# Token mix in 24 steps of all 512 channels, with products of 512 and 256 columns, in one fixed order that begins inside the attention's last units

## The chip, the core and the metric

The kernel runs on one core of one Trainium2 chip. The metric is the device time in microseconds (us) of one execution. The core's engines are TensorE (PE in the profile, its weight loads PEld), VectorE (DVE), ScalarE (ACT), GpSimd (POOL) and SyncE (SP, here only an issuer of DMAs). Each engine works through its own list of instructions in order and waits on semaphores for the others.

## The reference, cut to what matters

```python
scores = where(mask, q @ k.T / sqrt(64), -1e9)        # [4, 8, 768, 768], blocks of 32
x      = softmax(scores) @ v                          # attention, then [4, 768, 512]
theta  = x @ w_theta                                  # [4, 768, 512]
y      = w_tok_r @ (x * cos(theta)) + w_tok_i @ (x * sin(theta))   # mixes the 768 tokens
u      = x + y
out    = u + maximum(u @ w_ch, 0)
```

The mask keeps a window of three blocks, the first and the last block, and three sampled blocks for each block of queries. All inputs are float32.

## The kernel before, in words

**Attention.** The function `attention` runs over 56 units (two pairs of batches, each 6 units for the two edge blocks and 22 for the inner blocks), in an order that is written out by hand under a manual schedule. One unit has scores on PE (L315), row maxima on DVE (L323), exponentials on ACT (L341), transposes on PE (L351), their copies out of PSUM on ACT (L357), and products with the values on PE (L373, tile `X`); units overlap by a software pipeline, so that step n does the scores of unit n+1 and the values of unit n-1. The results go to a DRAM tile `xs` (L400). Weights arrive as 64-bit words; a `Decoder` turns them into a high and a low float32r part in "pieces": one activation and one cast on ACT (L63, L81) and seven DVE instructions (L68, L69, L70, L76, L78, L85, L86). A number of shares of pieces is due in each step of the attention; `theta`, all of `tok_r` and two thirds of `tok_i` are decoded there.

**Mix.** The function `token_mix` is a generator. It yields to the attention at its first loads, and then, in the attention's last step, at its first products. Everything after that is written in program order and put into its order on each engine by a scheduler of the framework that has a timeline of its own. There are 48 steps k: four batches b, two halves h of the 512 channels, six blocks j of 128 tokens. Each step loads `xa` (the block, turned) by four DMAs (L526); every other step loads `xr` (L537), turns it on DVE (`turn`, L553) and splits it into `xT` high and low (L554, L555). `theta(k)` makes 12 products of 256 columns (L563 to L565) into a PSUM tile `h`, and from it an angle between -pi and pi (ACT L567, L568; DVE L570 to L572) and its cosine and sine (ACT L574 to L576). `turned(k)` multiplies by `xa` (DVE L585) and splits both results into `zh` and `zl` (ACT L588, DVE L589). `mix(k)` makes 24 products of 384 columns (L601 to L603) into four PSUM tiles `y`, each of which collects all six blocks of its half. After j = 5, `add_x` adds x and splits the sum into `uh`, `ul` (DVE L614, L615, L617, ACT L616). `out` makes 12 products of 384 columns (L624 to L626), two DVE instructions (L629, L630) and a store; there are 32 of them, eight after each batch, those of the last batch at the very end. The 14 last pieces (six of 256 columns of `tok_i`, eight of `ch`) are decoded in the first steps of the mix. High and low parts mean three products for each full one: high by high, high by low, low by high.

**What is waited for around the change.** The pools of the mix (`zp`, `tp1`, `wk`, `up`, `ps_y`) lie where the attention's pools were, so their first use waits until those are released; `xp`, `tz` and `tp0` lie on the right side, in the place of the attention's early pools.

## Time and profile before

| | |
|---|---|
| median of 3 runs | 649.26 us (642.14 to 651.48) |
| the profiled execution | 649.64 us, of which 647.6 us are the span of its records |
| last value product of the attention starts | 286.50 us after the span's start |
| first product of `mix` | 306.97 us |
| last product of `out` starts | 643.49 us |

Busy time counts from the first to the last instruction of the span. Matmuls are pipelined, so the distance between the starts of two neighbours says more of PE's pace than the duration of one. The granted clock (PEclk) tells how much of full speed PE was given.

### The profile page before, as it was taken

Reading aid. Unit: us, or ns where it says so; the run is one execution under the profiler, and the core shown is the slowest. Engines: PE = TensorE matmul, PEld = TensorE weight load, DVE = VectorE, ACT = ScalarE, POOL = GpSimd, SP = SyncE. Lnnn points to the kernel's source line nnn. Section 1 sums busy time; section 2 is a strip of 40 time slices with the busy share of each in tenths; the row PEclk is TensorE's granted clock in tenths of the full one; section 3 lists DMA queues with packets and bytes.
Section 4 is the critical chain, followed back from the end, with each engine's and each line's share of the span. In section 5 each row is a group of like instructions: output and inputs, shape, how many; then the busy total and the mean of one; then the engine's idle time right before and its main releaser. Section 6 shows DMA issues by size and latency. Waiting matters only on the chain.

```text
span 647.6 us, 19671 instructions
## 1 busy us (share of the span) xinstructions
PE 560.7 (87%) x7936; PEld 489.0 (76%) x7936; DVE 460.6 (71%) x1207; ACT 356.8 (55%) x844; POOL 131.4 (20%) x230
## 2 busy tenths in 40 slices
PE   2788687698877787865999999999999999999997
PEld 1455465465555555654898989999999999999997
DVE  4677746568898677776889899674784857746554
ACT  1866666567866576754556655355552456424520
POOL 1248534352196454500000000000000000000000
PEclk9988988899988898987999999999999999999999
DMA  8937989968799788864442233311142211221002
GB/s 315 312 94 222 271 249 250 264 172 255 243 244 241 207 246 230 245 168 137 132 131 85 80 86 120 116 65 46 54 139 78 68 49 35 74 68 61 28 2 97
DMA packets 71098, 96.82 MB, mean 150 GB/s; under 512 B 5600, under 2 KB 52832, under 8 KB 70624
## 3 DMA queue, kind: packets, MB, share of 16 engines
q1 hardware_dynamic: 63488, 68.04, 35.6%
q0 software_dynamic: 4928, 17.57, 10.4%
q10 hardware_dynamic: 2592, 9.96, 5.1%
q8 instruction: 62, 1.02, 0.7%
q14 instruction: 28, 0.23, 0.1%
HBM read 82.97 MB, written 12.58 MB: 148 GB/s over the span
## 4 chain that ended last, share of the span: by engine, by line
PE 68%; DMA 13%; DVE 8%; issue 7%; ACT 3%; SPq 1%; DVEq 0%; ACTq 0%
PE X L373 8%; PE y L601 8%; PE y L603 8%; PE y L602 8%; PE S L315 7%; PE T L351 6%; PE o L624 3%; PE o L626 3%; PE o L625 3%; DMA raw_ch<-in_w_ch_dram 3%; PE h L565 2%; PE h L564 2%; PE h L563 2%; DMA xs<-xo 2%; PE X_w L373 2%
## 5 line engine op out<-in xcount | busy, mean ns | idle before, releaser
L601 PE MATMUL y<-w_second,zh 128*128 128x384 f32 x288 | 96.5, 335 | 1.2 <-ACT zh L588 1.2
L602 PE MATMUL y<-w_second,zh 128*128 128x384 f32 x288 | 96.3, 334 | 0.0
L603 PE MATMUL y<-w_second,zl 128*128 128x384 f32 x288 | 91.9, 334 | 0.0
L357 ACT COPY pT<-T 128x512 f32<-128x512 f32 x88 | 48.1, 590 | 60.6 <-PE T L351 59.3
L341 ACT ACTIVATE P<-S,nm 128x256 f32<-128x256 f32 x176 | 69.0, 476 | 11.0 <-DVE nm L325 10.0
L323 DVE TENSOR_REDUCE m<-S 128x2 f32<-128x512 f32 x88 | 56.6, 685 | 19.7 <-PE S L315 16.5
L373 PE MATMUL X<-vb,pT 128*32 128x65 f32 (+1 forms) x1408 | 58.5, 234 | 12.9 <-issue 11.9
L315 PE MATMUL S<-kg,q 64*32 64x256 f32 x1408 | 59.2, 405 | 10.5 <-issue 9.2
L373 PE MATMUL X<-va,pT 128*32 128x65 f32 (+1 forms) x1408 | 52.6, 237 | 14.4 <-DMA va<-in_vr_dram 5.1
L563 PE MATMUL h<-w_theta_hi,xTh 128*128 128x256 f32 x192 | 55.5, 289 | 10.5 <-ACT xTh L554 10.5
L351 PEld LDWEIGHTS T<-ident,P 128*128 128x128 f32 x352 | 42.0, 151 | 28.0 <-issue 14.1
L351 PE MATMUL T<-ident,P 128*128 128x128 f32 x352 | 56.7, 301 | 7.2 <-issue 5.7
L373 PEld LDWEIGHTS X<-va,pT 128*32 128x32 f32 (+1 forms) x1408 | 37.0, 117 | 26.2 <-issue 12.0
L565 PE MATMUL h<-w_theta_hi,xTl 128*128 128x256 f32 x192 | 55.7, 290 | 1.0 <-DVE xTl L555 1.0
L294 POOL DMA_INDIRECT vb<-in_vr_dram,rows x44 | 49.3, 1120 | 33.6 <-PE X_w L373 25.6
L601 PEld LDWEIGHTS y<-w_second,zh 128*128 128x128 f32 x288 | 54.1, 188 | 1.6 <-ACT zh L588 1.6
L373 PEld LDWEIGHTS X<-vb,pT 128*32 128x32 f32 (+1 forms) x1408 | 41.6, 119 | 17.9 <-issue 17.4
L564 PE MATMUL h<-w_theta_lo,xTh 128*128 128x256 f32 x192 | 55.1, 287 | 0.0
L602 PEld LDWEIGHTS y<-w_second,zh 128*128 128x128 f32 x288 | 54.1, 188 | 0.0
L603 PEld LDWEIGHTS y<-w_second,zl 128*128 128x128 f32 x288 | 53.7, 188 | 0.0
L567 ACT ACTIVATE t<-h,up_int 128x256 f32<-128x256 f32 x48 | 22.5, 472 | 48.1 <-PE h L565 40.9
L563 PEld LDWEIGHTS h<-w_theta_hi,xTh 128*128 128x128 f32 x192 | 37.5, 195 | 11.3 <-ACT xTh L554 11.3
(145 smaller groups left out, 1317.0 us busy)
## 6 DMA issues: line engine op xcount, KB each, us to landing
xa<-xs SPq DMA_DIRECT2D x192, 64.0 KB
va<-in_vr_dram SPq DMA_DIRECT2D x30, 260.0 KB
xr<-xs SPq DMA_DIRECT2D x24, 256.0 KB
out_dram<-of SPq DMA_DIRECT2D x32, 192.0 KB
q<-in_qT_dram SPq DMA_DIRECT2D x22, 256.0 KB
xs<-xo SPq DMA_DIRECT2D x44, 128.0 KB
raw_tok_r<-in_w_tok_r_dram ACTq DMA_DIRECT2D x8, 576.0 KB
va<-in_vr_dram SPq DMA_DIRECT2D x30, 130.0 KB
```

What stands on the lines that cost most here:

```text
L294: nc.gpsimd.indirect_dma_start(out=vb[0:96], out_offset=None, in_=vr, in_offset=bass.IndirectOffsetOnAxis(ap=tab.rows[:, bp, i : i + 1], a ...
L315: nc.tensor.matmul(sc[32 * p : 32 * p + 32, e, b, :], q[rows, b, p, :], keys[rows, :, 4 * b + p, :], start=True, stop=True)
L323: nc.vector.tensor_reduce(m[:, 2 * e : 2 * e + 2], sc[:, e], axis=AX.X, op=ALU.max)
L341: nc.scalar.activation(pt[:, e, b], sc[:, e, b], AF.Exp, bias=nm[:, 2 * e + b : 2 * e + b + 1], scale=0.125)
L351: nc.tensor.transpose(banks[k // 4][:, k % 4], pt[:, (k // 2) % 2, k % 2, 128 * (k // 4) : 128 * (k // 4) + 128], ident)
L373: nc.tensor.matmul(s["X"][32 * p : 32 * p + 32, b, e, :], s["T"][0:rows, 4 * c + 2 * e + b, 32 * p : 32 * p + 32], v[0:rows, v0 : v0 + 65] ...
L563: nc.tensor.matmul(ps, hi[:, c, :], wh[:, c, :], start=c == 0, stop=False)
L564: nc.tensor.matmul(ps, hi[:, c, :], wl[:, c, :], start=False, stop=False)
L565: nc.tensor.matmul(ps, lo[:, c, :], wh[:, c, :], start=False, stop=c == 3)
L601: nc.tensor.matmul(acc, zh[:, dd], wh[:, tt], start=j == 0 and m == 0, stop=False)
L602: nc.tensor.matmul(acc, zh[:, dd], wl[:, tt], start=False, stop=False)
L603: nc.tensor.matmul(acc, zl[:, dd], wh[:, tt], start=False, stop=j == 5 and m == 1)
```

## The change

In words:

- The mix has 24 steps (four batches, six blocks), each of all 512 channels. `theta(k)` is 12 products of 512 columns: first the eight with the high part of x, then the four with the low part. `mix(k)` is, for each of four blocks c of 128 channels, six pairs of products: 512 columns into a PSUM tile `ya` of its own, and 256 columns into a half of a PSUM tile `yb`, which the blocks 0 and 1, and the blocks 2 and 3, share. `out` is 12 pairs likewise, and for the last batch the eight outs stand side by side, with c as the outer loop.
- `xT` stays float32, and the high and low part of a block live in two short tiles. `add_x` adds in place (two DVE instructions of 512 and 256 columns), then one cast of 768 columns on ACT and one subtraction of 768 on DVE. `finish` is one DVE instruction instead of two.
- The whole mix is under a manual schedule: on each engine the instructions stand as the code has them. In step k stand `theta(k+2)`, the sines of k+1, `turn(k+3)`, the multiplications and splits of k+1, the integer and reduction of k+2, then 2, 2, 1, 1, 2, 1, 4, 1 pieces in the steps 0 to 7, then `mix(k)`, with four outs of the batch before between its second and third block of channels in the steps j = 1 and j = 2.
- The attention's early pools are released four units before its end, and the generator is called seven times from there to the last unit: raw loads, turns and splits of blocks 0 to 2, `theta(0)`, `theta(1)` and the reduction of block 0 stand inside the last units. The pieces of the attention are due four units before its end instead of one.
- The first two `xa` loads and the raw loads of all 14 last pieces are issued by GpSimd; before, SP issued them. The last outs are stored from SP (512 columns) and ACT (256).
- `xp`, `tz` and the raw tiles of the last pieces lie in the attention's main pools now.

The diff, cut to its core:

```diff
-                    due = 3 * len(early_pieces) + 3 * len(late_pieces) * (n - half) // (steps - 2 - half)
+                    due = 3 * len(early_pieces) + 3 * len(late_pieces) * (n - half) // (len(units) - 4 - half)
...
                 do(n - 1, values)
+                if len(units) - 2 <= n < len(units):
+                    next(follow)
                 do(n, evict)
...
+                if n == len(units) - 4:
+                    early.close()
+                if len(units) - 4 <= n < len(units):
+                    next(follow)
...
-        steps = 12 * nb
+        steps = 6 * nb
+        halves = ((0, 512), (512, 256))
...
-        def mix(k):
-            b, h, j = at(k)
+        def mix(k, between):
+            b, j = at(k)
             if j == 0:
-                ys[b, h] = [ps_y.tile([P, 384], F32, tag="y", name=f"y{k}_{a}") for a in range(4)]
-            for a in range(4):
+                two = [ps_y.tile([P, 2, 256], F32, tag=f"yb{x}", name=f"yb{b}_{x}") for x in range(2)]
+                ys[b] = [(ps_y.tile([P, 512], F32, tag=f"ya{c}", name=f"ya{b}_{c}"), two[c // 2][:, c % 2, :]) for c in range(4)]
+            for c in range(4):
...
+                if j == 5:
+                    add_x(b, c)
+                if c == 1:
+                    between()
...
+        def add_x(b, c):
...
+            u = xT[b][:, c, :]
+            for (t0, n), acc in zip(halves, ys[b][c]):
+                nc.vector.tensor_tensor(u[:, t0 : t0 + n], acc, u[:, t0 : t0 + n], op=ALU.add)
+            uh, ul = [t[:, c, :] for t in us[b]]
+            nc.scalar.copy(uh, u)
+            nc.vector.tensor_tensor(ul, u, uh.bitcast(F32), op=ALU.subtract)
...
+        def finish(b, e, t0, n, ps, queue):
+            o = wk.tile([P, 512], F32, tag="o", name=f"of{b}_{e}_{t0}")[:, :n]
+            nc.vector.scalar_tensor_tensor(o, ps, 0.0, xT[b][:, e, t0 : t0 + n], op0=ALU.max, op1=ALU.add)
+            queue.dma_start(outT[b, 128 * e : 128 * e + 128, t0 : t0 + n], o)
...
+        with tc.manual_schedule():
+            load(0, nc.gpsimd)
+            for piece in rest[:2]:
+                piece.load(stage, nc.gpsimd)
+            load(1, nc.gpsimd)
+            load_raw(4)
+            theta(2)
+            sines(0)
+            times(0)
+            split(0)
+            integer(1)
+            reduce(1)
+            load(2)
+
+            shares = [2, 2, 1, 1, 2, 1, 4, 1]
...
```

**PE at the attention's end** (tile names: `T` transposes, `X` value products, `h` the theta products, `xh` and `xl` the parts of x; the number behind `X_` is the block). Before, the last two units follow each other:

```order
L373 MATMUL X_20_5417<-vb_115,pT_20_5364 32x65 x4
L351 MATMUL T_22_0_5503<-ident,P_22_5453 128x128 x4
L351 MATMUL T_22_1_5504<-ident,P_22_5453 128x128 x4
L373 MATMUL X_21_5513<-va_113,pT_21_5450 32x65 x4
L373 MATMUL X_21_5513<-vb_116,pT_21_5450 32x65 x4
```

Now `theta(0)` stands between them, and `theta(1)` likewise ahead of `X_22`:

```order
L568 MATMUL h_5512<-w_theta_hi,xh_5482 128x512
L569 MATMUL h_5512<-w_theta_lo,xh_5482 128x512
L571 MATMUL h_5512<-w_theta_hi,xl_5483 128x512 x4
L351 MATMUL T_22_0_5532<-ident,P_22_5489 128x128 x4
L351 MATMUL T_22_1_5533<-ident,P_22_5489 128x128 x4
L373 MATMUL X_21_5542<-va_116,pT_21_5486 32x65 x4
```

What moved: 12 products of 512 columns ahead of the last transposes, and 12 more ahead of the last value products.

**GpSimd behind the attention's last gather** (`vb` are gathered values, `xa` the mix's blocks, `raw` the undecoded weights; what an instruction waits for is in brackets, DMAHW and DMASW being DMAs of the hardware and the software queues). Before, nothing follows:

```order
L259 COPY kg_110<-k_182 128x256 [waits Pool_49]
L294 DMA vb_116<-in_vr_dram,rows 96x1040 [waits DMASW6_49]
L294 DMA vb_117<-in_vr_dram,rows 96x1040 [waits DMASW7_49,PE_49]
L797 UNCONDITIONAL_BRANCH
L797 ISA [waits barrier_Pool_Activation_PE_DVE_SP_gather]
```

Now:

```order
L294 DMA vb_120<-in_vr_dram,rows 96x1040 [waits DMASW7_49,PE_49]
L535 DMA xa_5690<-xs 128x1x128 [waits DMAHW1_49,DMAHW0_49,DMAHW2_49,DMASW3_49,DMAHW3_49,DMASW2_49,DMAHW4_49,DMASW1_49,DMAHW5_49,DMASW0_49,DMAHW6_49,PE_49,DMAHW7_49,Activation_49,Pool_49]
L535 DMA xa_5690<-xs 128x1x128 x3
L58 DMA raw_tok_i_5695<-in_w_tok_i_dram 128x512
L58 DMA raw_tok_i_5697<-in_w_tok_i_dram 128x512
L535 DMA xa_5699<-xs 128x1x128 x2
```

What moved: eight `xa` loads and the raw loads came from SP's list to the end of GpSimd's. The first of them waits for PE's last value product `X_22`, since its tile lies in a pool that the attention releases as a whole.

**PE at the end of a batch, step 5, j = 5** (`y`, `ya`, `yb` are the sums in PSUM). Before, the four sums take turns and none waits for DVE's add:

```order
L601 MATMUL y_3_5816<-w_second,zh_5_6063 128x384
L602 MATMUL y_3_5816<-w_second,zh_5_6063 128x384
L603 MATMUL y_0_5813<-w_second,zl_5_6064 128x384 [waits DVE_49]
L603 MATMUL y_1_5814<-w_second,zl_5_6064 128x384
L603 MATMUL y_2_5815<-w_second,zl_5_6064 128x384
L603 MATMUL y_3_5816<-w_second,zl_5_6064 128x384
```

Now a block of channels is finished before the next begins:

```order
L627 MATMUL ya_0_5809<-w_second,zl_5_6244 128x512 [waits DVE_49]
L627 MATMUL yb_0_5807<-w_second,zl_5_6244 128x256
L627 MATMUL ya_1_5810<-w_second,zh_5_6239 128x512
L627 MATMUL yb_0_5807<-w_second,zh_5_6239 128x256 [waits DVE_49]
L627 MATMUL ya_1_5810<-w_second,zh_5_6239 128x512
```

What moved: the first product of block 1 into `yb_0` has a wait on DVE. It is the add that reads block 0's half of the same tile (the third row of the next list); before, `zl` was all that these products waited for.

**DVE in the same step** (`rr` the reduced angle, `da_ch`, `raw_ch`, `w_ch` a piece of the last weights):

```order
L586 TENSOR_SCALAR rr_6373<-rr_6373 128x512 [waits DVE_49]
L67 TENSOR_SCALAR da_ch_6377<-da_ch_6377 128x256 [waits Activation_49]
L68 TENSOR_SCALAR da_ch_6377<-da_ch_6377 128x256 [waits DVE_49]
L69 SCALAR_TENSOR_TENSOR da_ch_6377<-raw_ch_6265,da_ch_6377 128x256 [waits DMASW4_49,DVE_49]
L75 TENSOR_SCALAR ds_ch_6382<-da_ch_6377 128x256 [waits DVE_49]
L77 SCALAR_TENSOR_TENSOR raw_ch_6265<-raw_ch_6265,ds_ch_6382 128x256 [waits DVE_49]
L84 TENSOR_TENSOR da_ch_6377<-da_ch_6377,w_ch_hi 128x256 [waits Activation_49]
L85 TENSOR_TENSOR w_ch_lo<-da_ch_6377,raw_ch_6265 128x256 [waits DVE_49]
L642 TENSOR_TENSOR xT_5412<-ya_0_5809,xT_5412 128x512 [waits PE_49]
L642 TENSOR_TENSOR xT_5412<-yb_0_5807,xT_5412 128x256 [waits PE_49]
L645 TENSOR_TENSOR ul_6403<-xT_5412,uh_6402 128x768 [waits Activation_49]
```

Before, the adds stand among work of several steps:

```order
L69 TENSOR_SCALAR da_ch_6148<-da_ch_6148 128x256 [waits DVE_49]
L570 SCALAR_TENSOR_TENSOR rr_6308<-t_6305,h_6292 128x256 [waits DVE_49]
L614 TENSOR_TENSOR uf_0_0_0_6245<-y_0_5813,xTh_0_5595 128x384 [waits PE_49]
L572 TENSOR_SCALAR rr_6206<-rr_6206 128x256 [waits DVE_49]
L614 TENSOR_TENSOR uf_0_1_0_6256<-y_1_5814,xTh_0_5595 128x384 [waits PE_49]
```

What moved: the adds of a batch stand behind the whole of step 5's other DVE work, the reduction of block 7 and a piece included.

272 lines of the change are left out of this document (148 added, 124 removed).

## The prediction

> **What bounds the kernel now.** I read the page's busy shares and slices first, then the busy time by stage, then PE's list of instructions in time, then DVE's.
>
> ```profile
> PE 560.7 (87%) x7936; PEld 489.0 (76%) x7936; DVE 460.6 (71%) x1207; ACT 356.8 (55%) x844; POOL 131.4 (20%) x230
> PE   2788687698877787865999999999999999999997
> DVE  4677746568898677776889899674784857746554
> ```
>
> PE is the busiest engine, and from the nineteenth slice on it is nearly full: the attention ends there and the mix begins. By stage, where the first column is the stretch and the busy times of PE, PEld, DVE, ACT and POOL follow, then the granted clock:
>
> ```profile
> 287.00:307.00 20.00, 9.99 (x49) 8.88 (x50) 12.68 (x45) 7.96 (x20) 0.00 (x0) 0.79 0.52 151
> 307.00:347.00 40.00, 37.48 (x235) 36.67 (x235) 34.50 (x115) 23.51 (x61) 0.00 (x0) 0.98 0.44 123
> 347.00:400.00 53.00, 51.25 (x316) 49.98 (x315) 49.57 (x150) 32.05 (x84) 0.00 (x0) 1.00 0.30 88
> 400.00:629.30 229.30, 229.30 (x1437) 229.28 (x1436) 151.03 (x395) 108.06 (x256) 0.00 (x0) 1.00 0.21 65
> ```
>
> From 400 us on PE never pauses; only the first 113 us of the mix have room. PE's pace there comes from the first and the last of twelve products of 256 columns, and of twenty-four of 384:
>
> ```profile
> 440.04 0.28 PE L563 MATMUL h<-w_theta_hi,xTh 128*128 128x256 f32 x1
> ...
> 441.33 0.28 PE L565 MATMUL h<-w_theta_hi,xTl 128*128 128x256 f32 x1
> 441.44 0.34 PE L601 MATMUL y<-w_first,zh 128*128 128x384 f32 x1
> ...
> 445.43 0.34 PE L603 MATMUL y<-w_second,zl 128*128 128x384 f32 x1
> ```
>
> 1.29 us over 11 distances is 0.117 us for 256 columns, 3.99 over 23 is 0.1735 for 384: 0.44 ns a column and next to no fixed part. By that line 512 columns take 0.230 us. Before, the mix has 576 products of `theta` (67.4 us), 1152 of `mix` (199.9) and 384 of `out` (66.6), 333.9 us in all. The attention's last value product and the end of PE's list:
>
> ```profile
> 286.50 0.29 PE L373 MATMUL X<-vb,pT 96*32 96x65 f32 x8
> ...
> 643.49 0.34 PE L626 MATMUL o<-uh,w_ch_lo 128*128 128x384 f32 x1
> ```
>
> From 287.0 to 643.7 are 356.7 us, so waits and slow clock cost 22.8, nearly all before 400 us. That is all that a better order can win.
>
> **The change, part by part.** *Widths.* After, 288 products of 512 in `theta` (66.2 us), 576 pairs of 512 and 256 in `mix` (199.9; a pair is 0.347, two of 384 the same), 192 pairs in `out` (66.6): 332.7, a gain of 1.2 us. The number of columns is what PE pays for, and that stays.
>
> [...]
>
> *The waits before.* All 22.8 us go, to be replaced by those of the new order, which I work out one by one. T is the end of the attention's last value product.
>
> *Two thetas ahead of T.* `theta(0)` and `theta(1)` are 24 products, 5.5 us. They leave the mix, but stand in PE's list ahead of the last transposes and the last `X`, so T moves. In the last units PE had this gap, and over the attention's last 15 us these busy times:
>
> ```profile
> 281.37 0.32 PE L373 MATMUL X<-va,pT 128*32 128x65 f32 x8 [2.00 <-issue]
> ...
> 272.00:287.00 15.00, 11.88 (x352) 9.15 (x345) 11.63 (x28) 10.62 (x23) 1.69 (x2) 0.89 0.67 179
> ```
>
> Some of the 5.5 us fill such gaps: between 0 and 5.5 I take 2.5, as the gap is 2.0 and PE stood 15.0 - 11.9 = 3.1 us in the second row. Gain 3.0. On ACT the integer of block 0 goes ahead of the last copies of `T`, which wait for PE behind `theta(0)` anyhow; SP's raw loads stand ahead of the loads of `va`, which wait for an older `X` anyhow. The attention's pieces, due three units earlier, make room on DVE for the turns that come: 0.
>
> *The wait behind T.* GpSimd may issue `xa` only after T: four DMAs, then the landing. No row has a plain DMA of GpSimd; the nearest are its gathers and, for the landing, SP's load of the same data:
>
> ```profile
> L294 POOL DMA_INDIRECT vb<-in_vr_dram,rows x44 | 49.3, 1120 | 33.6 <-PE X_w L373 25.6 <-issue 6.2 <-PE X L373 1.5
> ...
> DMA to landing us min/median/max: 6.0/8.0/10.4
> 298.96 3.09 DMA xr<-xs
> 284.65 2.38 SPq L526 DMA_DIRECT2D xa<-xs  x4
> ```
>
> 4 x 1.12 + 2.7 (3.09 less the issue) is T+7.2. Then `times(0)` and the first cast; the rows for 512 columns:
>
> ```profile
> L555 DVE TENSOR_TENSOR xTl<-r,xTh 128x512 fp32r<-128x512 f32 x24 | 16.4, 685 | 2.7 <-ACT xTh L554 2.6
> L554 ACT CAST xTh<-r 128x512 fp32r<-128x512 f32 x24 | 14.8, 617 | 16.1 <-DVE r L553 15.6 <-DVE uf L614 0.6
> ```
>
> 0.69 + 0.62: `mix(0)` begins at T+8.5. `theta(2)` (2.8 us) covers a part; PE stands 5.7. Ends: SP's price for four issues (2.38) gives 3.6, the gathers' shortest landing of 6.0 gives 9.
>
> *DVE's queue against PE.* Per step DVE has four turns (0.88), two multiplications, `low`, two subtractions and three instructions of the reduction. Instructions that don't depend on their neighbour start closer together than those of a chain:
>
> ```profile
> 287.78 0.88 DVE L553 STREAM_TRANSPOSE r<-xr 128x128 f32<-128x128 f32 x4
> 342.75 0.42 DVE L589 TENSOR_TENSOR zl<-cs,zh 128x256 fp32r<-128x256 f32 x1
> 343.08 0.42 DVE L78 SCALAR_TENSOR_TENSOR raw_ch<-raw_ch,ds_ch 128x256 f32<-128x256 uint32 x1
> 443.15 0.42 DVE L571 SCALAR_TENSOR_TENSOR rr<-t,rr 128x256 f32<-128x256 f32 x1
> 443.61 0.29 DVE L572 TENSOR_SCALAR rr<-rr 128x256 f32<-128x256 f32 x1
> L68 DVE TENSOR_SCALAR da_tok_i<-da_tok_i 128x512 f32<-128x512 f32 x6 | 2.6, 426 | 0.2 <-issue 0.2
> L68 DVE TENSOR_SCALAR da_ch<-da_ch 128x256 f32<-128x256 f32 x8 | 2.3, 292 | 4.8 <-ACT da_ch L63 4.8
> L614 DVE TENSOR_TENSOR uf<-y,xTh 128x384 f32<-128x384 f32 x32 | 17.6, 552 | 11.8 <-PE y L603 11.7
> ```
>
> Neighbours start 0.33 apart, links of a chain 0.46. So a step is 0.88 + 5 x 0.64 + (0.69 + 0.69 + 0.43 + 0.1) = 6.0 us, and a piece, a chain of 3 x 0.29 and 4 x 0.42 with links, 2.6. PE's step is 2.76 + 8.33 = 11.1. With `split(0)` and the reduction of block 1 (three links and ACT's two ahead) DVE comes to step 0 at T+12.3. Ahead of the first add stand six steps and nine pieces, 36.0 + 23.4: T+71.7. PE ends block 0 of channels of step 5 at 8.5 + 5 x 8.33 + 5 x 2.76 + 2.08 = T+66.0. Its next product into `yb_0` waits for the adds of 512 (0.69) and 256 (0.42) columns: until 72.9, so 6.7 us. Before `yb_1` it waits once more: each block is two adds, ACT's cast of 768 (0.83 by the slope of its rows) and a subtraction (0.95), 2.9 us, against PE's 2.08; 1.7 us. Sum 8.4. Behind this wait stand the rest of step 5 and `theta(8)`, whose angles nobody needs yet.
>
> In step 6 DVE has the adds' end (T+84.3), a step and four pieces: T+100.7. PE is at the outs of step 7 at T+99.2. The first waits for the piece that holds its part of `ch` (1 us); the second waits for the `h` bank which the reduction of block 9 reads (a multiplication pair, splits and a turn further on, T+107: 4.5); the third for `finish` of the first, behind a last piece (3). Sum 8.5; queued behind are the rest of `mix(7)` and `theta(10)`.
>
> In later batches DVE has no pieces. Yet the reduction of k+2 ends 2.8 + 1.5 + 2.0 = 6.3 us into step j = 5 (`theta`, ACT's two, DVE's three), while block 0 ends at 4.8: 2.4 us, and 1.6 before `yb_1`; the last batch, without a theta, 2.6. Sum 10.6. For one such wait the floor is the two adds, 1.2 us, and the ceiling step 5's.
>
> *The tail.* Before, it is PE's last product and then:
>
> ```profile
> 632.07 1.02 DVE L630 SCALAR_TENSOR_TENSOR of<-o,of 128x384 f32<-128x384 f32 x2 [1.49 <-PE o L626]
> 634.62 1.03 DVE L629 TENSOR_TENSOR of<-uh,ul 128x384 f32<-128x384 f32 x2 [1.53 <-DMA out_dram<-of]
> 643.86 0.56 DVE L630 SCALAR_TENSOR_TENSOR of<-o,of 128x384 f32<-128x384 f32 x1 [0.63 <-PE o L626]
> ```
>
> A buffer `of` is free 2.0 us after its `finish` (632.6 to 634.6), and there are two of them still. Before, the outs end one by one, 2.1 us apart; now all eight end in the last 4.2 us, and every pair must wait for the stores of the pair ahead: 0.69 + 2.05 = 2.74 a pair. After the last mix: 12.5 (three quarters of the outs) + 0.9 + 3 x 2.74 + 1.1 + 3.2 (as before from the last `finish` to the end) = 25.9, against 16.6 + 3.9 = 20.5. A loss of 5.4.
>
> *The clock.* After a pause of 4.26 us PE ran at half speed:
>
> ```profile
> 303.57 0.58 PE L563 MATMUL h<-w_theta_hi,xTh 128*128 128x256 f32 x1 [4.26 <-ACT xTh L554]
> ...
> 307.29 0.52 PE L602 MATMUL y<-w_first,zh 128*128 128x384 f32 x1
> 307.61 0.52 PE L601 MATMUL y<-w_first,zh 128*128 128x384 f32 x1
> ```
>
> 0.32 us from start to start in place of 0.1735, until 308.9: 2.5 us lost. I expect three such pauses (behind T, in step 5, in step 7). What PE loses after the first shortens the wait for DVE in step 5, so I take 3.0 of 7.5, between 0 and 7.5. [...]
>
> *Sum*, against the execution's own time of 649.6 (span 647.6): - 22.8 - 1.2 - 3.0 + 5.7 + 8.4 + 8.5 + 10.6 + 5.4 + 3.0 = 664.2. The median of the runs, 649.26, is 0.4 below that execution; 664 is 2.3% above it.
>
> **The rivals.**
>
> *DVE keeps up.* If DVE's steps with pieces take 54 us instead of 59, step 5 costs 4.0 and step 7 nothing: 664.2 - 4.4 - 8.5 - 1 = 650.3, no change. For it: DVE's rows may pack closer under ACT's waits than I reckon. Against: they were 49.6 us busy of 53 in the stretch to 400 us, with the same pieces and less of a chain.
>
> *GpSimd's transfers are late.* If `xa` and the pieces land as the gathers do, 8 us after their issue, the start costs 5 more, and the third and fourth piece of step 6, loaded only within that step, hold DVE some 4 each: about 677. Against: those gathers ran while the DMA engines were busy; here the share is half. [...] The gathers' row shows no more than a mean of 1.12 us.
>
> *T moves by all 5.5 us*: 667.
>
> *Wide products are cheaper*, the case on the other side. If 512 columns take 0.203 us or less, the 1032 of them save 28 us, and the time falls to 636 or below, 2% under the median; at 384's price of 0.1735 it would be 606. No row has 512 columns in a stream; the straight line from 256 to 384 speaks against it. [...]
>
> **How the numbers follow.** The forecast's case, 664, spread from 655 to 672, has 0.53; DVE keeps up 0.20; late transfers 0.18; T moves fully 0.04; wide products 0.05. A measurement of this kernel can tell about 2% from no change, so slower means above 662.2. Three fifths of the forecast's case (0.32), late transfers and the moved T are slower: 0.54. The rest of it (0.21) and the case of 650 are the same: 0.41. Faster: 0.05. The range from 649 to 680 leaves out wide products and the outer parts of late transfers and of the case of 650, in all under 0.2.
>
> **What would show it.** In the profile after: products of 512 columns 0.23 us apart; PE idle some 6 us behind the last `X`, ended by ACT's `zh`; PE waits at `yb` that end with DVE's add, eight in all, the first the longest; waits of the outs in the second batch; DVE's `finish` waiting for `out_dram` at the end. A first add that finds PE still at work, or starts of 512 columns under 0.21 us apart, would make it wrong.

## The result and the profile after

The changed kernel takes 670.18 us (median of 4 runs, 666.27 to 675.15), the kernel before 648.31 (4 runs, 642.14 to 651.48); the ratio is 1.0353, with a 95% interval of 1.0237 to 1.047. Measured once more in a later set of runs it was 672.03 (6 runs) against 648.90, ratio 1.0344 (1.0295 to 1.0394). So it is slower, by 22 us where 15 were forecast, and inside the range of 649 to 680. The profiled execution took 673.61 us, its span is 671.8. In one later set of runs (e5 to e8) the ratios are taken against the lowest runs of the kernel before, of which one took 637.78 us, and come out about a per cent above those of the medians, so the medians are read there.

The busy engines and PE's share in the slices of the span, after:

```profile
PE 564.7 (84%) x7648; PEld 443.5 (66%) x7648; DVE 425.7 (63%) x959; ACT 327.3 (49%) x660; POOL 148.2 (22%) x252
PE   2877666777878778779997978998999997999994
```

PE's busy time is about the same (564.7 for 560.7); the span around it grew by 24 us. DVE and ACT do less than before (34.9 and 29.5 us), and that bought nothing: PE is the busiest engine in both kernels, and it now waits for the order in which the others work.

By stage, cut (within half a us) at the same distances behind the attention's last value product as in the prediction, and then the end; the columns are the stretch, the busy times of PE, PEld, DVE, ACT and POOL, and the granted clock:

```profile
292.00:312.00 20.00, 15.38 (x88) 12.69 (x77) 12.85 (x28) 9.96 (x18) 6.63 (x10) 0.83 0.44 126
312.00:352.00 40.00, 40.00 (x214) 34.04 (x213) 35.95 (x89) 23.78 (x43) 3.27 (x6) 1.00 0.34 92
352.00:405.00 53.00, 42.10 (x206) 35.00 (x204) 43.35 (x103) 25.20 (x46) 3.22 (x6) 0.90 0.21 61
405.00:634.00 229.00, 221.40 (x1174) 189.29 (x1175) 110.86 (x215) 78.57 (x123) 0.00 (x0) 0.98 0.15 49
634.00:671.80 37.80, 26.80 (x148) 22.14 (x146) 11.93 (x20) 3.33 (x4) 0.00 (x0) 0.95 0.11 42
```

Before, the first row was half a gap, the next two had 2.5 and 1.8 us of gaps, and the fourth was full. Now the first two are better (15.38 busy of 20, before 9.99; the second is full), and the third and fourth have gaps of 11 and 8 us. The fifth has 11 us, of which some 5 are the tail behind PE's last product, where 3.9 were before.

All waits of PE behind the last value product, by what ended them (total, count, longest):

```profile
PE yb L627 <- DVE xT L642: 14.8, 8, 4.6
PE ya L627 <- ACT zh L609: 4.6, 1, 4.6
PE o L651 <- DVE rr L584: 4.2, 1, 4.2
PE ob L651 <- DVE of L657: 3.3, 1, 3.3
PE o L651 <- DVE of L657: 1.7, 1, 1.7
```

Eight waits at `yb`, one pause ahead of mix(0), two waits of the outs in step 7, and one at the end: the places that the prediction named. In time, the first two and the two of step 7 stand here:

```profile
366.20 0.58 PE L627 MATMUL yb<-w_second,zh 128*128 128x256 f32 x1 [4.61 <-DVE xT L642]
373.67 0.39 PE L627 MATMUL yb<-w_second,zh 128*128 128x256 f32 x1 [0.93 <-DVE xT L642]
...
401.21 0.39 PE L651 MATMUL o<-uh,w_ch_hi 128*128 128x256 f32 x1 [4.24 <-DVE rr L584]
405.58 0.80 PE L651 MATMUL o<-uh,w_ch_hi 128*128 128x512 f32 x1 [1.69 <-DVE of L657]
```

PE's pace, from a place without waits (18 pairs of `mix` between the first two rows, a `theta` between the second and the third, three pairs of `out` between the last two):

```profile
480.75 0.40 PE L627 MATMUL ya<-w_first,zh 128*128 128x512 f32 x1
...
487.12 0.39 PE L568 MATMUL h<-w_theta_hi,xh 128*128 128x512 f32 x1
...
489.91 0.39 PE L627 MATMUL ya<-w_first,zh 128*128 128x512 f32 x1
...
649.77 0.40 PE L651 MATMUL oa<-uh,w_ch_hi 128*128 128x512 f32 x1
...
650.82 0.40 PE L651 MATMUL oa<-uh,w_ch_hi 128*128 128x512 f32 x1
```

A `theta` takes 2.79 us, so 512 columns take 0.2325. A pair of 512 and 256 takes 6.37/18 = 0.354 in `mix` and 1.05/3 = 0.350 in `out`, not the 0.347 of two products of 384.

The end of the attention, for which the prediction had taken 2.5 us. Here is DVE:

```profile
279.73 0.89 DVE L553 STREAM_TRANSPOSE xT<-xr 128x128 f32<-128x128 f32 x4 [4.61 <-DMA xr<-xs]
280.54 1.25 DVE L323 TENSOR_REDUCE m<-S 128x2 f32<-128x512 f32 x2
```

And SP's issue of the load that it waits for:

```profile
273.13 0.39 SPq L541 DMA_DIRECT2D xr<-xs  x1
```

The first turn of the mix stands in DVE's list ahead of the row maxima of the attention's last unit (L323). It waits 4.61 us for raw x, whose load was issued at 273.13 and had landed at 279.7. The maxima wait behind it, and with them the exponentials, the transposes and the last value product. ACT's list is held up likewise: its cast of the turned block waits 5.06 us, until 280.78, and stands ahead of ACT's last copies. The scores before, then scores and value products after, by their lines; the first and the last start stand behind the durations:

```profile
L315 PE MATMUL S<-kg,q x1408: 372/376/633, 39.1 to 277.3; 64*32 64x256 f32 x176
```

```profile
L315 PE MATMUL S<-kg,q x1408: 372/376/633, 36.9 to 274.9; 64*32 64x256 f32 x176
L373 PE MATMUL X<-vb,pT x1408: 217/220/318, 48.2 to 292.1; 128*32 128x65 f32 x168, 96*32 96x65 f32 x8
```

From the last scores to the last value product it was 9.3 us before (to 286.6), and is 17.2 now. GpSimd's transfers, on the other hand, were in time: four issues in 2.79 us (its list in time), and 3.1 to 4.1 us to the landing (the view of its line L535).

```profile
293.04 2.79 POOL L535 DMA_DIRECT2D xa<-xs  x4 [21.07 <-ACT cs L592]
```

```profile
DMA to landing us min/median/max: 3.1/3.3/4.1
```

The granted clock in four stretches, each behind one of PE's pauses (the seventh figure behind the stretch, after POOL's busy time):

```profile
299.90:306.70 6.80, 6.77 (x23) 5.80 (x24) 5.41 (x12) 4.79 (x9) 0.00 (x0) 0.55 0.37 105
366.20:371.20 5.00, 5.00 (x17) 4.28 (x18) 1.98 (x3) 1.15 (x2) 0.10 (x1) 0.54 0.18 52
401.20:412.20 11.00, 9.30 (x32) 7.89 (x33) 5.14 (x12) 2.18 (x4) 0.00 (x0) 0.53 0.15 52
466.40:470.20 3.80, 3.76 (x13) 3.24 (x14) 1.15 (x2) 0.83 (x1) 0.00 (x0) 0.55 0.02 4
```

Each of them ran at about half speed. What was lost is the busy time times what the clock lacked: 6.8 x 0.45 + 5.0 x 0.46 + 9.3 x 0.47 + 3.8 x 0.45 = 11.4 us.

### The profile page after: what moved, and what is told of

Same layout as the page of the kernel before. It is cut to its first block, busy times and chain, and to the rows that moved or that the text cites. A ratio compares the mean times of both kernels' runs of the same rounds, so it can differ in the third digit from the quotient of the medians.

```text
span 671.8 us, 18527 instructions
## 1 busy us (share of the span) xinstructions
PE 564.7 (84%) x7648; PEld 443.5 (66%) x7648; DVE 425.7 (63%) x959; ACT 327.3 (49%) x660; POOL 148.2 (22%) x252
## 4 chain that ended last, share of the span: by engine, by line
PE 50%; DVE 14%; DMA 3%; ACT 3%; issue 2%; POOL 0%; DVEq 0%; SPq 0%; ACTq 0%
PE ya L627 18%; PE yb L627 9%; PE h L568 3%; PE h L569 3%; PE h L571 3%; PE o L651 2%; PE o L652 2%; PE o L653 2%; DVE m L323 2%; DVE xT L642 2%; PE X L373 2%; PE S L315 1%; PE T L351 1%; DMA va<-in_vr_dram 1%; DMA xr<-xs 1%
## 5 line engine op out<-in xcount | busy, mean ns | idle before, releaser
L627 PE MATMUL ya<-w_second,zh 128*128 128x512 f32 x288 | 110.0, 404 | 0.0
L627 PE MATMUL yb<-w_second,zh 128*128 128x256 f32 x288 | 83.0, 288 | 14.8 <-DVE xT L642 14.8
L323 DVE TENSOR_REDUCE m<-S 128x2 f32<-128x512 f32 x88 | 56.4, 683 | 20.7 <-PE S L315 20.6
L627 PEld LDWEIGHTS yb<-w_second,zh 128*128 128x128 f32 x288 | 56.0, 194 | 17.8 <-DVE xT L642 17.3
L627 PEld LDWEIGHTS ya<-w_second,zh 128*128 128x128 f32 x288 | 55.7, 193 | 13.9
L627 PE MATMUL ya<-w_second,zl 128*128 128x512 f32 x144 | 58.9, 409 | 0.0
L584 DVE SCALAR_TENSOR_TENSOR rr<-t,h 128x512 f32<-128x512 f32 x24 | 16.5, 688 | 45.1 <-ACT t L578 45.1
L315 PEld LDWEIGHTS S<-kg,q 64*32 64x32 f32 x1408 | 24.2, 112 | 31.2 <-issue 21.0
L627 PE MATMUL yb<-w_second,zl 128*128 128x256 f32 x144 | 41.3, 287 | 0.0
L627 PE MATMUL ya<-w_first,zh 128*128 128x512 f32 x96 | 36.9, 408 | 4.6 <-ACT zh L609 4.6
L568 PE MATMUL h<-w_theta_hi,xh 128*128 128x512 f32 x96 | 39.3, 409 | 1.6 <-ACT xh L557 1.6
```

The costliest lines, as they stand in the source:

```text
L315: nc.tensor.matmul(sc[32 * p : 32 * p + 32, e, b, :], q[rows, b, p, :], keys[rows, :, 4 * b + p, :], start=True, stop=True)
L323: nc.vector.tensor_reduce(m[:, 2 * e : 2 * e + 2], sc[:, e], axis=AX.X, op=ALU.max)
L568: nc.tensor.matmul(ps, hi[:, c, :], wh[:, c, :], start=c == 0, stop=False)
L584: nc.vector.scalar_tensor_tensor(r, t, -C1, ps, op0=ALU.mult, op1=ALU.add)
L627: nc.tensor.matmul(acc, z[:, dd], wt[:, t0 : t0 + n], start=first and (n == 512 or c % 2 == 0), stop=last, skip_group_check=n == 256,)
```

## The experiments

The kernels were run in four sets, each set beside the kernel before on the same chip. That kernel's medians in the four sets are 649.89 (e1 to e4), 647.30 (e5 to e8), 647.57 (e9, e10) and 648.90 (e11, e12), so medians of different sets may be compared to some 2 us. Runs of one kernel spread over 5 to 15 us, and by an estimate from the profiles below much of that is the attention's end and the stretches at half clock. So for waits the traces decide, and for the total the medians.

### 1. The order of blocks at the end of a batch (e2)

```diff
-            for c in range(4):
+            for c in (0, 2, 1, 3) if j == 5 else range(4):
```

> In step j = 5 the blocks of channels go 0, 2, 1, 3 instead of 0, 1, 2, 3, so that the two halves of one tile yb no longer follow each other; nothing else. Theory (PE waits for the add that reads the other half): the eight waits at yb, 14.8 us in all, fall to 3.3 + 0.7 + 0.7 + 0 = about 4.7, and the stretch at half clock behind those of 2 us goes: 10 to 12 us faster than the changed kernel, near 659, ratio to before 1.017. Rival 1 (DVE's lag is the limit, the wait only moves): the waits at yb fall likewise, but the wait in step 7 grows from 5.9 to 9 or more, and the time falls by 7. Rival 2 (not the shared tile): waits and time as they were.

Measured: 656.78 us (655.13 to 659.83), ratio 1.0131 (1.0055 to 1.0208): 13 us off the changed kernel's 670. The waits of PE that differ, and that for the reduction in step 7:

```profile
PE o L651 <- DVE rr L584: 4.2, 1, 4.2
PE yb L627 <- DVE xT L642: 3.4, 3, 2.5
...
PE o L651 <- DVE of L657: 1.4, 1, 1.4
PE o L651 <- ACT w_ch_hi L80: 0.8, 1, 0.8
PE o L653 <- DVE w_ch_lo L85: 0.4, 1, 0.4
```

The waits at `yb` fall from 14.8 to 3.4; in step 7 they grow by 0.9 only (0.8 and 0.4 are new, 1.7 became 1.4), so they do not move there. Some 10.5 us of waits are thus gone by this one line of order; the 13 of the median may hold some of the attention's end too, whose last value product came at 288.4 in this profile for 292.1. The theory holds, and both rivals fall: of the waits won at `yb` less than a tenth came back in step 7.

### 2. The outs in one step (e3)

```diff
-                    for _ in range(4 if j in (1, 2) else 0):
+                    for _ in range(8 if j == 2 else 0):
```

> All eight outs of a batch stand in step j = 2 instead of four in j = 1 and four in j = 2; nothing else. Theory (in step 7 PE waits for DVE, which is late by the pieces of that step and the one before; one step on it has caught up): the waits of 4.24 and 1.69 us in step 7 go, and with them the stretch at half clock that follows, worth some 4 us: 8 to 10 us faster than the changed kernel, near 661, ratio to before 1.02. Rival (DVE is late for the rest too): a wait of 4 us or more appears in step 8 at the outs or at a product of mix, and the time falls by less than 3.

Measured: 668.50 us (660.84 to 672.42), ratio 1.0318 (1.0232 to 1.0404). In its trace the waits of the outs fell from 5.9 to 2.2:

```profile
PE o L651 <- DVE rr L584: 1.5, 1, 1.5
PE o L651 <- DVE of L657: 0.7, 1, 0.7
```

The wait did what the theory said, but the median shows 2 us of the 8 to 10. Two of the four runs (660.84 and 665.67) lie 9.3 and 4.5 us below the changed kernel's median, the other two (671.34 and 672.42) above it, so with this spread neither no gain nor the full one can be excluded. That the time follows is not shown by this run. What can be said is that PE's wait of 4 us did not reappear in step 8.

### 3. The last finishes in place (e4)

```diff
-            o = wk.tile([P, 512], F32, tag="o", name=f"of{b}_{e}_{t0}")[:, :n]
+            if b == nb - 1:
+                o = xT[b][:, e, t0 : t0 + n]
+            else:
+                o = wk.tile([P, 512], F32, tag="o", name=f"of{b}_{e}_{t0}")[:, :n]
```

> The last batch's finish writes into xT in place and is stored from there, so that it needs no buffer of the two; nothing else. Theory (the pairs at the end stand 2.84 us apart because each waits for the stores of the pair before): they come 1.05 us apart, PE's last wait of 3.3 us goes, the time from the last product of mix to the end falls from 26 to 21.5: 4.5 us faster than the changed kernel, near 665.5, ratio to before 1.028. Rival (the stores are what is slow): the stores queue up, 2 us faster or less.

Measured: 662.38 us (657.44 to 666.84), ratio 1.0226 (1.0133 to 1.032). DVE's last two finishes of 512 columns, first in the changed kernel, then here:

```profile
664.75 0.69 DVE L657 SCALAR_TENSOR_TENSOR of<-oa,xT 128x512 f32<-128x512 f32 x1 [1.82 <-DMA out_dram<-of]
667.58 0.69 DVE L657 SCALAR_TENSOR_TENSOR of<-oa,xT 128x512 f32<-128x512 f32 x1 [1.80 <-DMA out_dram<-of]
```

```profile
650.36 0.69 DVE L660 SCALAR_TENSOR_TENSOR xT<-oa,xT 128x512 f32<-128x512 f32 x1 [0.27 <-PE oa L653]
651.41 0.69 DVE L660 SCALAR_TENSOR_TENSOR xT<-oa,xT 128x512 f32<-128x512 f32 x1
```

From 2.83 apart to 1.05, no wait for `out_dram`, and PE's last wait of 3.3 us is gone. The eight stores of these finishes, issued within some 4 us, are no limit, so the rival falls. The median gained 8 us where 4.5 were expected. The 3.5 above that are within the runs' spread (in this profile the last value product also came early, at 286.3, with less of the half clock behind it: a granted clock of 0.96 in the 40 us from 340 us on and in the 40 from 380, for 0.91 and 0.87), and nothing shows that they belong to the end.

### 4. The thetas behind the attention (e1, e5, e6)

In e1 the two thetas were written into the mix's first lines; the framework moved them back among the attention's last products, so that the kernel hardly differs from the changed one.

```diff
         yield
-        theta(0)
         high(1)
         low(1)
-        integer(0)
         yield
-        theta(1)
-        reduce(0)
         yield
...
             load_raw(4)
+            theta(0)
+            integer(0)
+            reduce(0)
+            theta(1)
+            high(2)
+            low(2)
             theta(2)
```

> Both thetas that the change put into the attention (of blocks 0 and 1) stand behind its last value product, with what hangs on them. Theory: in the profile of the changed kernel they cost the attention all of their length and a stretch at half clock (8 us from the last scores to the last value product more than before), and PE then stood 4.6 us anyhow; without them the last value product starts 8 us earlier against the last scores, mix(0) follows it by 9 us instead of 7.4, PE hardly pauses there and no half clock follows (3 us): about 8.5 us faster than the changed kernel, near 661, ratio to before 1.02. Rival, the prediction's own pricing (the last value product moves by 2.5 us only, the thetas' 5.6 us of work then stand in the mix, mostly in the pause): no change, near 670, ratio 1.035.

Measured: 666.31 us (662.71 to 669.29); the distance from the last scores to the last value product was 17.7 us. Nothing follows for the theory. In e5 and e6 one more call of the generator, behind the last value product within the attention's own fixed order, holds the thetas there:

```diff
-                if len(units) - 2 <= n < len(units):
+                if len(units) - 2 <= n <= len(units):
                     next(follow)
```

> The first try left the thetas where they were: the framework put them back among the attention's last products. Here they are written into the attention's own fixed order, behind its last value product. Theory: from the start of the last scores to the last value product it was 9.3 us before, and 12.5 to 17.2 us in the four profiles with both thetas ahead of it; now it is about 9.5. PE does three thetas behind it, mix(0) starts 9.2 us behind it (theta, integer, reduction, sines, multiplication, cast) instead of 7.4, PE waits there less than 1 us instead of 4.6, and the granted clock behind mix(0)'s start stays at 1: 4 to 6 us faster than the changed kernel, ratio to before 1.026 to 1.029. Rival (the prediction's pricing: the thetas were half hidden by gaps of the attention): the last value product comes 2.5 us earlier, mix(0) 0.7 us earlier, ratio 1.034.

Measured: 664.88 us (661.00 to 667.64). Both halves of the expectation on the end of the mix's start came (mix(0) 9.6 us behind the last value product, PE's wait there 0.7 us), but the distance from the last scores stayed at 14.0 us instead of 9.5. So the thetas were not what had stretched the attention most. The median is 5 us below the changed kernel's, as expected, but only part of the expected path is there.

> As the run before, but only theta(1) goes behind the last value product, theta(0) stays ahead. Theory: theta(1) ran at full speed without a gap ahead of the last value product, so that comes 2.8 us earlier (about 10 to 14 us behind the last scores' start), and theta(1) fills the pause: PE waits 1.8 us instead of 4.6, mix(0) still starts 7.4 us behind the last value product, the clock stays up: 3 to 6 us faster than the changed kernel, ratio 1.026 to 1.031. Rival as before: within 1 us of the changed kernel.

Measured: 669.31 us (665.12 to 671.63), no gain. The distance was 15.4 us, mix(0) came 9.2 us behind the last value product instead of 7.4, and PE's pause was still 3.2 us. The theory fails here too. The changed kernel has 7.8 us there (the table below), and the 1.4 us more lie in GpSimd's first loads of `xa`: their issue began 0.9 us behind the last value product's start in both, but the first multiplication stood 6.9 us behind that issue for 5.5. Why they landed later stays open.

These two misses led to the DVE row quoted above. Here are the wait of the first turn for raw x, and the distances, from all profiles in which the turn stands at its place (e8 and e11 are told of below); `X` and `S` are the starts of the last value product and of the last scores, and the column `theta(0)` runs from its first product to the transposes behind it:

| kernel | turn waits | theta(0) | S to X | X to mix(0) | S to mix(0) |
|---|---|---|---|---|---|
| before (no turn ahead of the last maxima) | - | - | 9.3 | | |
| e4 | 2.4 | 2.9 | 12.5 | 7.9 | 20.4 |
| e2 | 2.8 | 2.9 | 12.9 | 7.8 | 20.7 |
| e3 | 3.1 | 2.9 | 13.8 | 7.9 | 21.7 |
| changed, second profile (e11) | 4.0 | 4.4 | 16.4 | 7.7 | 24.1 |
| e1 | 4.2 | 5.5 | 17.7 | 7.7 | 25.4 |
| changed | 4.6 | 4.7 | 17.2 | 7.8 | 25.0 |
| e7 | 5.3 | 4.5 | 17.7 | 7.7 | 25.4 |
| e6 (theta(1) behind) | 4.6 | 5.3 | 15.4 | 9.2 | 24.6 |
| e8 (theta(1) behind) | 4.9 | 5.3 | 15.6 | 9.2 | 24.8 |
| e5 (both thetas behind) | 5.1 | - | 14.0 | 9.6 | 23.6 |

Take 9.3 and the turn's wait away, and the first seven have 0.8, 0.8, 1.4, 3.1, 4.2, 3.3 and 3.1 us left for the thetas, the three below them 1.5 and 1.4 (one theta) and -0.4 (none). The wait for the load is thus the larger part, 2.4 to 5.3 us of a stretch of 3.2 to 8.4. The rest goes with the pace of `theta(0)`: in e2, e3 and e4 its products started 0.23 us apart and it took 2.9 us, and the rest is 0.8 to 1.4; in the other four it took 4.4 to 5.5, and the rest is 3.1 to 4.2. Of these four, the changed kernel and e1 had its products 0.43 us apart, in the changed kernel at a granted clock of 0.50 from 278.67 to 285.49 us.

### 5. The turns later (e9)

Besides e5's edit, the first turn stands behind the last unit's maxima, and the casts behind the last copies on ACT:

```diff
         load_raw(1)
+        yield
+        yield
         turn(0)
-        yield
-        high(0)
-        low(0)
-        yield
-        turn(1)
         load_raw(2)
         yield
...
+        high(0)
+        nc.scalar.activation(early, half_pi, AF.Sin)
+        low(0)
+        turn(1)
+        load_raw(3)
         high(1)
         low(1)
```

> As e5_thetas_behind_2, and besides the first turn stands on DVE behind the row maxima of the attention's last unit instead of ahead of them, the casts of x on ACT behind the last copies, the second and third turn later too. New theory for the attention's end: in the changed kernel's profile DVE stood 4.61 us (5.14 in e5) at the first turn, which waits for the load of raw x, issued 6 us before it landed; the last unit's maxima, exponentials, transposes and value product are queued behind it. Without it the last value product starts 9 to 10.5 us behind the last scores' start, as before the change, instead of 14.0 in e5; mix(0) 9.2 to 10.5 us behind that; 4 us faster than e5, so near 661, ratio to before 1.02. Rival (the thetas' and casts' place was the cause, or the loads themselves, which share the DMA engines): the distance stays at 12.5 or more, and the time at that of e5.

Measured: 664.98 us (661.74 to 667.74), ratio 1.0277 (1.0206 to 1.0347). DVE no longer waits for the load, only ACT's last copy holds the turn back a little; but a new wait of PE comes up:

```profile
279.36 0.89 DVE L553 STREAM_TRANSPOSE xT<-xr 128x128 f32<-128x128 f32 x4 [0.97 <-ACT pT L357]
```

```profile
294.03 0.50 PE L568 MATMUL h<-w_theta_hi,xh 128*128 128x512 f32 x1 [3.16 <-ACT xh L557]
```

The last value product stands 10.1 us behind the last scores, as expected. So the mechanism is shown: the turn's wait ahead of the attention's work, not the loads' share of the DMA engines. What DVE's list and what ACT's had of it is not separated, since the turn and the cast moved together. And the time did not follow: theta(2) now waits for its own turn, and mix(0) starts 12.6 us behind the last value product, 22.7 us behind the last scores. One wait replaced another.

### 6. The pause filled (e7)

```diff
             theta(2)
+            spare = ps_y.tile([P, 512], F32, tag="ya3", name="spare")
+            for x in range(18):
+                nc.tensor.matmul(spare, w["theta"][0][:, 0, 0:128], w["theta"][0][:, 0, :], start=x == 0, stop=x == 17)
```

> Eighteen products of 512 columns that nobody reads (4.2 us, into the sum of block 3 before its first product overwrites it) fill PE's pause between theta(2) and mix(0); nothing else. Theory (the half clock behind mix(0)'s start comes from the pause of 4.6 us): mix(0) starts 7.4 us behind the last value product as before, PE waits less than 0.7 us there, the granted clock in the ten us that follow is 1.00 instead of 0.65 to 0.85, and the first step is 1.7 to 3.4 us shorter: ratio to before about 1.032. Rival (the clock falls for another reason, such as the start of wide products): the half clock stays, and the ratio is 1.035.

Measured: 664.67 us (664.03 to 668.88). The stretch behind mix(0)'s start, to be held against the first of the four above, and PE's waits up to 400 us:

```profile
294.90:301.70 6.80, 6.76 (x38) 5.83 (x39) 5.40 (x12) 4.79 (x9) 0.00 (x0) 1.00 0.39 111
```

```profile
PE yb L627 <- DVE xT L642: 7.0, 2, 5.5
...
PE ya L627 <- ACT zh L609: 0.4, 1, 0.4
```

38 products instead of 23 in 6.8 us, at a clock of 1.00 instead of 0.55: the pause is the cause of the half speed. Of the 3.1 us won, 1.5 go back at once: the waits of step 5 grow from 5.5 to 7.0 us, since PE comes earlier to a DVE that is no earlier. The median is 5.5 us below the changed kernel's; only some 2 of these can belong to the edit.

The same pause does not always cost the same. Behind a wait of 2.04 us in the second batch the changed kernel ran at 0.55 (the fourth of the stretches above); e1, behind the same wait, ran at full speed:

```profile
460.84 0.39 PE L627 MATMUL yb<-w_second,zh 128*128 128x256 f32 x1 [2.04 <-DVE xT L642]
```

```profile
460.80:464.60 3.80, 3.76 (x22) 3.29 (x23) 1.98 (x3) 1.47 (x2) 0.00 (x0) 1.00 0.02 4
```

What decides between the two is not shown. In the changed kernel the granted clock was 0.50 from 299.15 to 305.97 us, from 364.00 to 370.83, from 401.55 to 411.79 and from 466.40 to 469.81: 6.82, 6.83, 10.24 and 3.41 us, at or behind the pauses of 4.62, 4.61, 4.24 and 2.04 us.

### 7. Together (e8, e10, e12), and the changed kernel again (e11)

e8 has the edits of e2, e3, e4 and e6.

> All together: theta(1) behind the last value product, blocks of channels in the order 0, 2, 1, 3 in step j = 5, all outs in step j = 2, and the last finishes in place. Theory (the terms are separate waits of PE, and each is gone by itself): behind the last value product remain theta 2 x 2.8, a pause of 1.8, 24 mixes of 8.45, 21 thetas of 2.79, 192 pairs of 0.353 and some 7 us of waits and end, 345 us in all against 379.6 in the changed kernel's profile; with the last value product at 286 to 289 the execution takes 633 to 638 us, ratio to before 0.975 to 0.985, so faster than both. Rival (DVE's lag is one resource: what one wait gives up the next takes): waits of 5 us or more appear in the steps 6 to 9, and the ratio is 1.00 or above.

Measured: 646.66 us (10 runs, 637.54 to 652.07), ratio 0.9964 (0.9896 to 1.0033): 23.5 us below the changed kernel, and the time of before (647.30), not less. Behind the last value product remained 355.6 us, not 345; in its trace the waits at `yb` are 3.3 us, the pause at the start 3.1 (1.8 expected), the outs 1.8 and a new wait of 1.1 for a cast. No wait of 5 us appeared, so the waits are mostly separate, as the theory had it; its sum left out what stays of the half clock.

e10 has e9's start in place of e6's, and one more edit:

```diff
-                for _ in range(shares.pop(0) if shares else 0):
+                def pieces():
+                    nonlocal done
+                    for _ in range(shares.pop(0) if shares else 0):
...
+                if j != 5:
+                    pieces()
...
                 mix(k, outs)
+                if j == 5:
+                    pieces()
```

> e9_turns_later, with the order 0, 2, 1, 3 in step j = 5, the outs in step j = 2, the last finishes in place, and the pieces of step 5 behind that step's adds on DVE. Against e8_all_four (355.6 us from the last value product's start to the end, of it 3.1 at the start, 3.3 at yb, 1.8 in step 8 and some 5 of half clock): the start and yb waits fall under 1 us each and the half clock behind them goes, while theta(0) comes in (2.8): about 350 us; and the last value product comes 4 us earlier by the theory of e9. Theory: 7 to 10 us faster than e8, 637 to 640, ratio to before 0.983 to 0.99, faster than both kernels. Rival 1 (the attention's end is not shortened): 643, ratio 0.993. Rival 2 (the piece moved behind the adds makes DVE late in steps 6 to 8): a wait of 4 us or more at the outs of step 8, ratio 1.00.

Measured: 641.61 us (6 runs, 638.24 to 643.45), ratio 0.9894 (0.9843 to 0.9945): faster than the changed kernel, and faster than the one before by 1.1%, less than the 2% that the prediction took a measurement to tell, though the interval leaves out 1. Part of rival 2 came true:

```profile
PE h L568 <- ACT xh L557: 7.7, 2, 4.6
PE yb L627 <- DVE xT L642: 1.3, 3, 0.4
```

The waits at `yb` are all but gone, but the piece moved behind step 5's adds makes DVE late for the cast of block 10, and `theta(10)` waits 4.6 us for it (the other 3.15 are those of e9).

e12 is e10 with the third turn and its cast ahead of the first reduction and of theta(1):

```diff
         theta(0)
-        integer(0)
-        reduce(0)
-        theta(1)
         turn(2)
+        integer(0)
         high(2)
+        reduce(0)
         low(2)
+        theta(1)
```

> e10_all_five, with the third turn and its cast ahead of the first reduction and of the second theta. In e9 and e10 PE waited 3.16 and 3.15 us for the cast of block 2, whose turn stood on DVE behind the reduction of block 0, which waits for theta(0) and ACT. Theory: that wait goes, mix(0) is bound by the chain of block 0 alone and starts 10 us behind the last value product's start instead of 12.6 (e9: 296.93 against 284.3) and 13.2 (e10: 296.8 against 283.6), and no half clock follows: 2 to 4 us faster than e10, near 638.5, ratio 0.985, faster than both kernels. Rival (the second theta, now queued behind more, is late for block 1 and the wait moves into step 0): no gain, ratio 0.99.

> The changed kernel once more, unedited, as the base on the same chip for the run beside it and for the spread of its attention's end. Theory: the distance from the last scores' start to the last value product's start is 9.3 us (before) plus DVE's wait for the raw load of x at the first turn (2.4 to 5.3 us in the seven profiles that keep that turn there) plus 1 to 3.3 us for the two thetas; so between 12.5 and 18, and PE's other waits stay as they were: 4.6 at the start, 5.5 + 3.5 + 3.5 + 2.2 at yb, 4.2 + 1.5 in step 7, 3.3 at the end. Time 665 to 672, ratio to before 1.03 to 1.035. Rival (the wait for the load was a single event): a distance below 11.

Measured on one chip: e12 640.17 us (6 runs, 636.48 to 645.04), ratio 0.9878 (0.9833 to 0.9923); the changed kernel 672.03, ratio 1.0344 (1.0295 to 1.0394). In e11 the turn waited 4.0 us, the distance was 16.4, and PE's waits were 4.5, 15.3, 4.2, 1.4 and 3.3: as expected, and not a single event. In e12 mix(0) starts 9.5 us behind the last value product, with a pause of 0.7 us, and what is left of PE's waits is this:

```profile
PE h L568 <- ACT xh L557: 4.6, 1, 4.6
PE yb L627 <- DVE xT L642: 2.2, 4, 0.9
PE o L651 <- DVE of L660: 0.9, 1, 0.9
PE ya L627 <- ACT zh L609: 0.7, 1, 0.7
PE ob L651 <- DVE xT L642: 0.2, 1, 0.2
```

8.6 us of 28.6. Against e10 it gained 1.4 us in the median, less than the spread; against before, e12 is faster by 1.2%, and its interval leaves out 1. A kernel with the change's 24 steps and its widths is thus no slower than the old one, although its pairs of products cost some 4 us more (the table below). Most of what cost 22 us was the order, and at the end the two buffers.

## Why the prediction was right

The direction and the places were right; the size was low, 15 of 22 us in the medians. The terms, against the profiled execution (span 647.6 to 671.8, 24.2 more):

| term | predicted | measured | from |
|---|---|---|---|
| waits of the old order | -22.8 | -22.8 | the prediction's rows |
| widths | -1.2 | +4.2 | 576 x 0.354 + 192 x 0.350 + 288 x 0.2325, less 333.9 |
| thetas out of the mix | -5.5 | -5.6 | 24 x 0.2325 |
| the attention's end | +2.5 | +7.9 | 17.2 - 9.3 |
| the attention ahead of it | 0 | -2.4 | last scores at 274.9 for 277.3 |
| pause ahead of mix(0) | 5.7 | 4.6 | wait rows |
| step 5 at `yb` | 8.4 | 5.5 | 4.61 + 0.93 |
| step 7, outs | 8.5 | 5.9 | 4.24 + 1.69 |
| later batches at `yb` | 10.6 | 9.3 | 14.8 - 5.5 |
| the end | 5.4 | 5.7 | last mix product at 645.6 to 671.8, against 20.5 |
| half clock | 3.0 | 11.4 | the four stretches |
| sum | 14.6 | 23.7 | |

Point by point:

- **The wait behind T.** Right in kind. mix(0) came 7.6 us behind the end of the last value product (292.3) for 8.5 forecast. The rival with late GpSimd transfers fell: 3.1 to 4.1 us to the landing. The issues took 0.70 us each, less than the 1.12 of the gathers.
- **DVE against PE in step 5.** The first product behind the add was forecast for 72.9 us behind T and came at 73.9; PE stood ready at 69.3 and not at 66.0, mostly since it had lost 3 us at half speed. The prediction had said that what PE loses ahead shortens this wait, and e7 showed the same in reverse. e2 showed that the shared tile is the cause.
- **Step 7.** The `h` bank behind the reduction of block 9 was right to 0.3 us (4.24 for 4.5); the wait for the first piece did not appear, and that for `finish` was 1.7 for 3.
- **Later batches and the end.** Right within 1.3 and 0.3 us; e4 showed the two buffers to be the cause of the latter.
- **Mis-sized: the attention's end.** The step that failed is "The attention's pieces, due three units earlier, make room on DVE for the turns that come: 0." The room was there, but the turn is not only work. It waits for a load, and stands in DVE's list ahead of the last unit's maxima; the wait was 4.61 us here, 2.4 to 5.3 in all profiles, and e9 took it away. "T moves by all 5.5" was given 0.04 as a rival, and the stretch was in fact 3.2 to 8.4 us longer in the seven profiles with both thetas ahead. In absolute time the last value product came 5.5 us later here (292.1 for 286.6), the rival's number but not by its mechanism. The last scores came 2.4 us earlier; whether by the edit or by chance stays open, as they start at 269.5 to 276.1 in all thirteen profiles of kernels with the new attention and at 277.3 in the only one of before.
- **Mis-sized: the clock.** 3.0 of a ceiling of 7.5, measured 11.4. Three pauses were counted; there were four with half clock behind them, for 6.82, 6.83, 10.24 and 3.41 us at 0.50, so by an estimate from these each cost up to half its length, 1.7 to 5.1 us. The term also has a spread: in e3's profile the clock was 0.93 in the 20 us from 280 us on, 0.99 in the 40 us behind those, 0.96 in the next 40 and 1.00 from there to 640; an estimate from these is two stretches of some 3.6 and 3.2 us.
- **Mis-sized: the widths.** The price of 512 columns was right (0.2325 for 0.230), that of 256 too. What was not foreseen is that the alternating pair takes 0.354; why it does stays open. The rival of cheap wide products fell.

The errors have both signs: the waits for DVE and GpSimd came out 7.9 us lower together, the clock 8.4, the widths 5.4 and the attention's end 5.4 higher, with 2.4 given back ahead of it. So the waits were priced too high and partly hid that three other terms were priced too low; that the total fell inside the range owes something to this luck.

## What to carry to other kernels

When sums of several blocks share one PSUM tile, look at which block follows which on TensorE: with the neighbour in the same tile, the next block waits for the add of the one before, and changing the order of four numbers was worth 13 of 22 us in the medians; the trace shows 10.5 us of waits gone. When work of a next stage is slipped into a full stage's fixed order, price not only its length on each engine but what it waits for, since everything behind it in that engine's list waits too. And if a new order brings pauses of 2 to 5 us on TensorE, add the half clock behind them to the sum, as a term that varies from run to run: here it was 11.4 us behind four pauses of 2.04 to 4.62 us in the changed kernel's profile, and none behind the pause of 2.04 us in e1's.

## What the runs showed of the hardware

- Products of 512 and 256 columns in alternation take 0.354 us a pair where 0.2325 + 0.117 = 0.350 were to be expected from products of one width, and two of 384 take 0.347.
- A pause of 4.6 us was followed by half speed for 6.8 us in one profile (granted clock 0.55), and by full speed in another in which it was filled (1.00); a pause of 2.04 us was followed by it for 3.41 us in one profile, at 0.50, and not in another (e1, at 1.00). In the changed kernel this is 11.4 us behind four pauses, 1.7% of the time.
- A load of 128 x 512 values by SP took 6.2 us from the end of its issue to the wait's end, in a part of the attention where the DMA engines' share was 0.83 (270 to 280 us), while the plain loads of GpSimd behind the attention, a quarter of that size each, landed in 3.1 to 4.1 at a share of 0.44.
